# An adaLN decode block: attention in units of two kv heads, with fewer and larger loads

## The chip, the core and the metric

The kernel runs on one core of one Trainium2 chip. The core has a matrix engine (TensorE, PE in the profile, its weight loads PEld), a vector engine (VectorE, DVE), a scalar engine (ScalarE, ACT), a general engine (GpSimd, POOL) and a queue engine (SyncE, SP) that issues most transfers. Sixteen DMA engines move data between the main memory and the on-chip memory SBUF, which has 128 partitions. Matrix products land in a second memory, PSUM, and are read from there by DVE and ACT. Each engine runs its own instructions in the order in which they stand, and waits on semaphores for the others. The metric is the device time of one execution in microseconds (us), less is better.

## What is computed

Two tokens (B = 2, one position each) pass through an attention block and a feed-forward block. Both are modulated by a condition `c`. All numbers are float32.

```
mod = (silu(c) @ w_mod) -> sa, ca, ga, sb, cb, gb          # w_mod 512 x 3072
h = layernorm(x) * (1 + ca) + sa
q = h @ wq                                                 # 512 x 4096: 32 heads of 128
k, v = the last 4096 of 32768 cache rows, 8 kv heads       # 4 query heads share a kv head
o = softmax(q k^T / sqrt(128)) v ;  x = x + ga * (o @ wo)  # wo 4096 x 512
h = layernorm(x) * (1 + cb) + sb
x = x + gb * (silu(h @ w1) @ w2)                           # w1 512 x 1792, w2 1792 x 512
```

Nearly all bytes are read once: 16 pairs of batch and kv head, each with 2 MB of keys and 2 MB of values (67.1 MB), and 30.4 MB of weights, 97.5 MB in all.

## The kernel before

The kernel is written with a tile layer that makes the semaphores. Most instructions may be moved by its scheduler; those wrapped in `inorder(...)` keep the order in which they are written, on each engine.

**Loads.** All large loads go through SP's queue, in order. Their targets are tiles of a ring of eight (`RING = 8`, `stream()`), each 128 partitions by 16 KB, 2 MB. `load_rows` brings `w_mod` in four pieces and `wq` in four. `load_k` and `load_v` bring one head's keys or values of one batch: partition p holds 32 consecutive cache rows, 16 KB in one run. `load_runs` brings `wo`, `w1` and `w2`; the end of `w2` is cut into eight small pieces. A load may start when the ring's tile is free, that is, when the last reader of what lay there is done.

**Head.** `m_ch` and `m_sp` are products of `silu(c)` with `w_mod`, four of each per piece, as each piece lands. The queries (`q`, line 271) are 32 products of 512 columns, eight for each of the four pieces of `wq`. They are turned by DVE (`qT`, line 280), spread out (`qg`), repeated by a product (`qr`, line 288) and copied into `qbd` (line 294), the weights of the score products.

**Attention.** `seq` has 16 units t, one kv head of one batch each. For a unit:

- `keys` (line 352): DVE turns the keys in 32 x 32 blocks, four instructions of 128 x 1024, into `kT`.
- `scores` (line 368): 16 products of 256 columns into `s`. They stand in four groups of 32 output rows; products for different groups run side by side in the array.
- `maxima` (line 378): DVE takes each row's maximum `mx`; a product with the identity turns it into a row `mT` (line 460); `maxrow` reduces it (`mg`, line 384) and spreads it (`mrow`, line 390); a product (`bp`, line 398) makes a column of it, ACT copies it to `bias` (line 400).
- `exponentials` (line 402): ACT computes `pr = exp(scale * s + bias)` and its row sums.
- `turn` (lines 414, 416): DVE turns `pr` into `xp` and spreads it with a mask into `zp`.
- `permute` (lines 426, 433): four products gather it into `pT`, ACT copies that to `ptb`.
- `weighted` (lines 313, 322): eight products of 512 columns of values into `o`, in two parts of four; ACT copies `o` to `ob`.
- `collect` (line 328): four products of 128 columns, one for each group of output rows, add the unit's result to `o_all`.

The loop over t works on two units at a time: it turns the keys and makes the scores of unit t between the softmax and the weighting of unit t - 1. `kT` has two buffers (`ktp`, bufs=2), each of a whole unit.

**End.** The row sums give `lp` and `rl`; `on` and `oTn` are the scaled and turned result. `acc_o` (line 545, 24 products of 512 columns) and `ao` (line 554, 32 of 128) are the product with `wo`, joined by `gather` (line 532). Then follow the second layer norm in a transposed form (`aoT`, `x1T`, `mean`, `dT`, `hT`), the product with `w1` (`hid`, line 586), the activation (`hidT`, `z`, `sgh`, `uT`), the product with `w2` (`acc_yw`, line 619, and `acc_y`, line 629), two instructions for `yo`, and the store.

Of the kernel before, what the change touches and what calls it, by code (L numbers as in the profile page):

```python
# [16 lines left out]
G = HQ // HKV  # L17
F = 1792
EPS = 1e-5
RING = 8  # L20
# [3 lines left out]
def adaln_block(  # L24
# [19 lines left out]


# [4 lines left out]
    assert W == 4096  # L50


    head = ctx.enter_context(tc.tile_pool(name="head", bufs=1))
    id4 = head.tile([P, 32], F32, name="id4")
    ring = ctx.enter_context(tc.tile_pool(name="ring", bufs=RING))
# [5 lines left out]
    psum1 = ctx.enter_context(tc.tile_pool(name="psum1", bufs=1, space=bass.MemoryType.PSUM))  # L61

# [6 lines left out]
    def stream(name):  # L69
        return ring.tile([P, 4096], F32, tag="st", name=name)  # L70

    def load_rows(name, w, k, width):
        t = stream(f"{name}{k}")[:, :width]
        nc.sync.dma_start(t, w[k * P : (k + 1) * P, :])  # L74
        return t

    def load_k(b, h):
        t = stream(f"k{h}_{b}")
        nc.sync.dma_start(
            t, k_cache[b, h, SK - W :, :].rearrange("(p n) d -> p (n d)", p=P)  # L80
        )
        return t

    def load_v(b, h):
        t = stream(f"v{h}_{b}")
        nc.sync.dma_start(
            t, v_cache[b, h, SK - W :, :].rearrange("(p n) d -> p (n d)", p=P)
        )
        return t

    def load_runs(name, w, per, lo, hi):

        e = w.shape[1]
        t = stream(f"{name}{lo}")[:, : (hi - lo) * e].rearrange("p (q e) -> p q e", e=e)
        nc.sync.dma_start(t, w.rearrange("(p q) e -> p q e", q=per)[:, lo:hi, :])
        return t


    x2 = x.rearrange("b s d -> (b s) d")
    x_sp, x_ch, c_ch = const([P, P], "x_sp"), const([P, P], "x_ch"), const([P, P], "c_ch")  # L100
    for t in (c_ch, x_ch, x_sp):
        nc.vector.memset(t, 0.0)
    wm = [load_rows("wm", w_mod, 0, 6 * D)]
    rows8 = lambda t: t.rearrange("(ab r) m -> ab r m", r=16)[:, 0, :]
    for t, src in ((c_ch, c), (x_ch, x2)):
        for b in range(B):
            nc.sync.dma_start(
                rows8(t)[b : 2 * 4 : 2, :].rearrange("a (k c) -> a k c", k=4),
                src[b, :].rearrange("(k a c) -> a k c", k=4, a=4),
            )  # L110
# [61 lines left out]
    for t in ptb:  # L172
        nc.gpsimd.memset(t[:, P:], 0.0)
# [132 lines left out]
    def weighted(t, vt, part):  # L306


        if part == 0:
            o_ps[t] = bank("D", f"o{t}")  # L310
# [359 lines left out]
```

## Time and profile before

| quantity | value |
|---|---|
| median of 3 runs | 240.01 us (239.88 to 241.7) |
| span of the profiled execution, first to last instruction | 238.5 us |
| mean granted TensorE clock in it | 0.843 of full speed |
| records of PE | 1476, two for each of 738 float32 products |
| DVE, busy | 118.4 us, 212 instructions |
| ACT, busy | 35.2 us, 96 instructions |

The profile gives no time for the profiled execution other than its span; the median of the runs is 1.5 us above it, which stands for what lies around the span.

How to read what the prediction quotes: a page has the busy time of each engine, the span in 40 slices of 6 us (a digit is the busy share in tenths, PEclk the granted clock in tenths), the DMA queues, the chain of work that ended last, and the costliest groups of instructions. A row of a group reads: line, engine, operation, output <- input, shapes and count, then the busy time of the group in us and the mean of one in ns, then the idle time before them and what ended it. In rows of the timeline and of the chain the first number is the start in us from the span's start and the second the duration. "128\*32" is a product that takes 128 rows and 32 columns of the array.

### The profile page before, as it was taken

How to read it: one execution, taken by the hardware profiler on the slowest of the kernel's cores; microseconds unless marked ns; L12 is line 12 of the kernel's file. 1: busy time of each engine (PE TensorE's matmuls, PEld its weight loads, DVE VectorE, ACT ScalarE, POOL GpSimd, SP SyncE). 2: the span in 40 equal slices, each digit the busy share in tenths (PEclk: the TensorE clock that was granted, in tenths of full speed). 3: DMA queues.
4: the chain of work that ended last, by engine and by line, in shares of the span. 5: the costliest groups of instructions: out<-in, count | busy, mean ns of one | idle time of the engine just before them, and what ended most of it. 6: DMA issues, size and time to landing. Idle time of an engine off the chain costs nothing.

```text
span 238.5 us, 3514 instructions
## 1 busy us (share of the span) xinstructions
PE 163.8 (69%) x1476; PEld 64.3 (27%) x1476; DVE 118.4 (50%) x212; ACT 35.2 (15%) x96; POOL 9.3 (4%) x30
## 2 busy tenths in 40 slices
PE   0194656386987696787585967869759687776854
PEld 0131101122333132342231322414323131315212
DVE  0604001759687847649477485584864912101130
ACT  2300000103112202202112021120211211020200
POOL 8400000100000000000000000000000000000000
PEclk9999577766799977979979779797997897797779
DMA  6999999999999999999999999999999999999970
GB/s 243 428 429 431 431 429 440 426 427 431 426 434 431 423 434 426 434 429 434 426 429 434 430 426 431 431 429 430 426 431 430 429 437 426 420 430 425 419 247 20
DMA packets 7783, 97.75 MB, mean 410 GB/s; under 512 B 968, under 2 KB 984, under 8 KB 1752
## 3 DMA queue, kind: packets, MB, share of 16 engines
q1 hardware_dynamic: 7768, 97.54, 96.6%
q8 instruction: 11, 0.18, 0.3%
q14 instruction: 4, 0.03, 0.0%
HBM read 97.53 MB, written 0.00 MB: 409 GB/s over the span
## 4 chain that ended last, share of the span: by engine, by line
DMA 71%; DVE 17%; PE 8%; ACT 1%; issue 1%; SPq 1%; POOL 0%; POOLq 0%
DMA k<-in_A_k_cache_dram 42%; DVE kT L352 14%; DMA w<-in_B_w_dram 13%; DMA wq<-in_A_wq_dram 13%; PE s L368 4%; DMA wm<-in_w_mod_dram 3%; PE o L313 2%; DVE qT L280 1%; DVE mx L378 1%; SPq L74 1%; PE q L271 0%; DVE mrow L390 0%; DVE qbd L294 0%; PE pT L426 0%; DVE zp L416 0%
## 5 line engine op out<-in xcount | busy, mean ns | idle before, releaser
L352 DVE STREAM_TRANSPOSE kT<-k 128x1024 f32<-128x1024 f32 x64 | 75.5, 1215 | 16.0 <-DMA k<-in_A_k_cache_dram 16.0
L368 PE MATMUL s<-kT,qbd 128*32 128x256 f32 x512 | 69.7, 518 | 10.0 <-DVE kT L352 9.5
L313 PE MATMUL o<-v,ptb 128*32 128x512 f32 x256 | 35.2, 627 | 5.7 <-ACT ptb L433 5.7
L368 PEld LDWEIGHTS s<-kT,qbd 128*32 128x32 f32 x512 | 23.8, 140 | 46.5 <-DVE kT L352 29.9
L378 DVE TENSOR_REDUCE mx<-s 128x1 f32<-128x256 f32 x16 | 6.8, 425 | 30.0 <-PE s L368 30.0
L398 PE MATMUL bp<-negscale,mrow 1*128 1x1 f32 x32 | 6.5, 268 | 21.6 <-DVE mrow L390 21.6
L271 PE MATMUL q<-wq,hq_T 128*32 128x512 f32 x64 | 11.4, 847 | 9.7 <-DMA wq<-in_A_wq_dram 9.7
L322 ACT COPY ob<-o 128x512 f32<-128x512 f32 x16 | 9.4, 585 | 37.5 <-PE o L313 37.5
L398 PEld LDWEIGHTS bp<-negscale,mrow 1*128 1x128 f32 x32 | 5.1, 198 | 35.5 <-DVE mrow L390 35.5
L433 ACT COPY ptb<-pT 128x128 f32<-128x128 f32 x16 | 4.2, 265 | 66.1 <-PE pT L426 66.1
L328 PE MATMUL o_all<-ob,selh 128*32 128x128 f32 x128 | 13.2, 308 | 1.1 <-ACT ob L322 0.7
L426 PE MATMUL pT<-zp,id 128*32 128x128 f32 x128 | 13.5, 304 | 0.2 <-DVE zp L416 0.2
L416 DVE TENSOR_TENSOR zp<-xp,group 128x512 f32<-128x512 f32 x16 | 11.1, 693 | 0.5
L313 PEld LDWEIGHTS o<-v,ptb 128*32 128x32 f32 x256 | 7.8, 111 | 11.6 <-ACT ptb L433 10.3
L280 DVE STREAM_TRANSPOSE qT<-q 128x512 f32<-128x512 f32 x2 | 1.4, 717 | 18.8 <-PE q L271 18.5
L328 PEld LDWEIGHTS o_all<-ob,selh 128*32 128x32 f32 x128 | 8.0, 130 | 4.3 <-ACT ob L322 2.1
L426 PEld LDWEIGHTS pT<-zp,id 128*32 128x32 f32 x128 | 7.9, 127 | 1.0 <-issue 0.5
L402 ACT ACTIVATE pr<-s,bias 128x256 f32<-128x256 f32 x16 | 7.6, 474 | 0.7 <-ACT bias L400 0.2
L414 DVE STREAM_TRANSPOSE xp<-pr 128x256 f32<-128x256 f32 x16 | 6.4, 397 | 2.2 <-ACT pr L402 2.2
L271 PEld LDWEIGHTS q<-wq,hq_T 128*32 128x32 f32 x64 | 2.1, 130 | 19.0 <-DMA wq<-in_A_wq_dram 11.4
L545 PE MATMUL acc_o<-wo,oTn 128*32 128x512 f32 x48 | 6.9, 729 | 0.4 <-DVE oTn L523 0.4
L203 PE MATMUL mean_a<-mv_a,avg 128*128 128x1 f32 x2 | 0.6, 361 | 9.4 <-DVE mv_a L200 9.4
(126 smaller groups left out, 100.6 us busy)
## 6 DMA issues: line engine op xcount, KB each, us to landing
k<-in_A_k_cache_dram SPq DMA_DIRECT2D x16, 2048.0 KB
v<-in_A_v_cache_dram SPq DMA_DIRECT2D x16, 2048.0 KB
wq<-in_A_wq_dram SPq DMA_DIRECT2D x4, 2048.0 KB
wo<-in_A_wo_dram SPq DMA_DIRECT2D x4, 2048.0 KB
wm<-in_w_mod_dram SPq DMA_DIRECT2D x4, 1536.0 KB
w<-in_B_w_dram SPq DMA_DIRECT2D x2, 1024.0 KB
w<-in_B_w_dram SPq DMA_DIRECT2D x1, 1792.0 KB
w<-in_B_w_dram SPq DMA_DIRECT2D x2, 896.0 KB
```

What stands on the lines that cost most here:

```text
L271: nc.tensor.matmul(q_ps[n][32 * g : 32 * g + 32, :], hq_T[:, k, :], wv[:, n, g], start=(k == 0), stop=(k == 3),)
L313: inorder(nc.tensor.matmul(o_ps[t][32 * c : 32 * c + 32, :], ptb[t % 2][:, 16 * n : 16 * n + 32], vt[:, 512 * n : 512 * n + 512], start=(p ...
L322: inorder(nc.scalar.copy(sb_, o_ps[t]))
L328: inorder(nc.tensor.matmul(o_all[32 * m : 32 * m + 32, b, :], selh[:, m, HQ - G - G * h : 2 * HQ - G - G * h], o_sb[:, m * DH : (m + 1) * DH],
L352: inorder(nc.vector.transpose(kT[t][:, :, 8 * n4 : 8 * n4 + 8, :].rearrange("p j n k -> p n j k"), kt[t][:, n4 * 1024 : (n4 + 1) * 1024].r ...
L368: inorder(nc.tensor.matmul(s_ps[t][32 * cc : 32 * cc + 32, :], qbd[h // 4][:, h % 4, b, j, :], kT[t][:, j, 8 * cc : 8 * cc + 8, :], start= ...
L378: inorder(nc.vector.tensor_reduce(mx[t], s_ps[t], axis=AX.X, op=ALU.max))
L398: inorder(nc.tensor.matmul(bp[:, 0:1], mrow[t % 2], negscale, start=True, stop=True))
L402: inorder(nc.scalar.activation(pr[t].rearrange("p s k -> p (s k)"), s_ps[t], AF.Exp, bias=bias, scale=SCALE, accum_out=rowsum[:, h, b : b ...
L416: inorder(nc.vector.tensor_mul(zp, xp[:, None, :, 0:16].to_broadcast([P, 4, 8, 16]), group[:, :, None, None].to_broadcast([P, 4, 8, 16]),))
L426: inorder(nc.tensor.matmul(tp[32 * i : 32 * i + 32, :], id4, zp.rearrange("p c s x -> p (c s) x")[:, :, 4 * i : 4 * i + 4], start=True, st ...
L545: nc.tensor.matmul(acc[32 * g : 32 * g + 32, :], oTn[:, q, :], wot[q // 8][:, q % 8, :], start=(q < 4), stop=(q >= 20),)
```

## The change

The attention, its buffers and all large loads are written anew.

- **Buffers.** One tile `store` of 128 partitions by 144 KB replaces the ring. It holds four slots of 32 KB a partition (4 MB each) and a spare part for small tiles. At first `wq` lies in slots 0 and 1, and `w_mod` in slot 3 and the spare part.
- **Loads.** `w_mod` (6.3 MB) and `wq` (8.4 MB) are one load each. A unit is a batch and two kv heads, so there are 8 units; `load_cache` brings both heads' 4 MB at once: partition p holds 64 consecutive cache rows (one run of 32 KB) of head p mod 2. Keys of units 0, 2, 4, 6 go to slot 2 and values to slot 3; those of units 1, 3, 5, 7 to slots 0 and 1. `wo` is three loads, `w1` three, `w2` four of 128 partitions each. `x` and `c` come through ACT's queue, once each.
- **Head.** The products with `w_mod` and `wq` begin when the whole matrix has landed. The layer norm works on the same layout for both blocks, which saves a few small DVE instructions.
- **Attention.** `attend(t)` holds a whole unit, and the loop calls it for one unit after another; the part of unit t no longer stands between parts of unit t - 1. DVE turns the keys in four instructions of 128 x 2048. After each, four score products of 512 columns follow. They read `kT[:, 32f:32f+32, u:32:2]`, every second element, to pick head u. `kT` is now a quarter of a unit and has two buffers, so the third of the four instructions waits for the scores of the first. `mx`, `pr`, `xp` and the two `zp` work on 512 columns; `pT` has four products of 256 columns; `ptb` is made by two ACT instructions with a mask `par`; `o` has 16 products. After every second unit `o_all` gets four products of 256 columns that all write the same 32 output rows.
- **End.** `on` and `oTn` are made by DVE alone (`rq`, `on`, a reduction), without the four `oq` products. The rest is as before.

Of two engines it is shown how their order changes. First PE at the middle of the attention. Before, `s_415` are the scores of one unit, and `pT_375`, `o_381` belong to the unit ahead of the one whose scores are `s_355`:

```order
L398 MATMUL bp_343<-negscale,mrow_145 128x1
L368 MATMUL s_355<-kT_337,qbd_153 32x256 x16
L426 MATMUL pT_375<-zp_353,id_58 32x128 x4
L313 MATMUL o_381<-v_0_305,ptb_147 32x512 x4
L460 MATMUL mT_374<-ident,mx_372 1x128
L313 MATMUL o_381<-v_0_305,ptb_147 32x512 x4
L398 MATMUL bp_403<-negscale,mrow_146 128x1
L368 MATMUL s_415<-kT_397,qbd_153 32x256 x16
```

The same place on PE now, from the second unit (`s_341`) to the start of the third (`s_413`):

```order
L292 MATMUL s_341<-kT_342,qbd_124 32x512 x4
L292 MATMUL s_341<-kT_348,qbd_124 32x512 x4
L292 MATMUL s_341<-kT_354,qbd_124 32x512 x4
L292 MATMUL s_341<-kT_360,qbd_124 32x512 x4
L302 MATMUL mT_368<-ident,mx_366 1x128
L319 MATMUL bp_374<-negscale,mrow_121 128x1
L334 MATMUL pT_382<-store,sel 32x256 x4
L350 MATMUL o_389<-store 32x512 x16
L360 MATMUL o_all<-store,pick 32x256 x4
L292 MATMUL s_413<-kT_414,qbd_124 32x512 x4
```

Before, a unit's scores stand ahead of the weighting `o` of the unit before it; now all 16 products of `o`, and in every second unit the four of `o_all`, stand ahead of the next unit's first scores.

DVE before, where `mx_436` belongs to the unit with the keys `k_0_333` and everything with `xp` and `zp` to the unit ahead of it:

```order
L352 STREAM_TRANSPOSE kT_397<-k_0_333 128x8x4x32 x2
L414 STREAM_TRANSPOSE xp_411<-pr_407 128x256
L416 TENSOR_TENSOR zp_413<-xp_411,group 128x512
L378 TENSOR_REDUCE mx_436<-s_415 128x1
L352 STREAM_TRANSPOSE kT_461<-k_1_393 128x8x4x32 x2
L384 TENSOR_REDUCE mg_464<-mT_438 1x4
L390 COPY mrow_145<-mg_464 1x4x16
L352 STREAM_TRANSPOSE kT_461<-k_1_393 128x8x4x32 x2
```

DVE now, from the last turn of one unit's keys (`kT_292`) through that unit's softmax to the third turn of the next (`kT_354`); the tiles in `store` are `xp` and `zp`:

```order
L287 STREAM_TRANSPOSE kT_292<-store 128x2048
L300 TENSOR_REDUCE mx_298<-s_273 128x1
L304 TENSOR_REDUCE mg_302<-mT_300 1x8
L314 COPY mrow_120<-mg_302 1x2x16 x2
L325 STREAM_TRANSPOSE store<-store 128x512
L327 TENSOR_TENSOR store<-store,half 128x512 x2
L287 STREAM_TRANSPOSE kT_342<-store 128x2048
L287 STREAM_TRANSPOSE kT_348<-store 128x2048
L287 STREAM_TRANSPOSE kT_354<-store 128x2048
```

Before, DVE turns keys of the next unit while PE and ACT work on the maximum and the exponentials; now it goes through a unit's whole softmax, from `mx` to the second `zp`, before it turns any key of the next.

The diff, cut to the loads, the attention and the head's queries:

```diff
-RING = 8
+SLOT = 8192
...
+    store = big.tile([P, 36864], F32, name="store")
+    slot = [store[:, i * SLOT : (i + 1) * SLOT] for i in range(4)]
...
-    wm = [load_rows("wm", w_mod, 0, 6 * D)]
+    wm = store[:, 24576:36864].rearrange("p (k e) -> p k e", k=4)
+    nc.sync.dma_start(
+        wm.rearrange("p k e -> p (k e)"), w_mod.rearrange("(p k) e -> p (k e)", k=4)
+    )
...
-    wqt = [load_rows("wq", wq, k, HQ * DH) for k in range(4)]
+    wqt = store[:, :16384].rearrange("p (k e) -> p k e", k=4)
+    nc.sync.dma_start(
+        wqt.rearrange("p k e -> p (k e)"), wq.rearrange("(p k) e -> p (k e)", k=4)
+    )
...
+    def load_cache(cache, t, where):
+        hp, b = seq[t]
         nc.sync.dma_start(
+            where,
+            cache[b, 2 * hp : 2 * hp + 2, SK - W :, :].rearrange(
+                "u (i n) d -> i u (n d)", n=NK
+            ),
+        )
+        return where
...
+    def attend(t):
+        hp, b = seq[t]
+        s_ps = bank("A", f"s{t}")
+        kv = kt[t].rearrange("p (n j r) -> p n j r", n=NK, j=4)
         for j in range(4):
+            kT = ktp.tile([P, NK, 32], F32, tag="kT", name=f"kT{t}")
+            inorder(nc.vector.transpose(kT, kv[:, :, j, :]))
+            for u in range(2):
+                h = 2 * hp + u
+                for f in range(2):
+                    r = 32 * (2 * u + f)
+                    inorder(nc.tensor.matmul(
+                        s_ps[r : r + 32, :],
+                        qbd[h // 4][:, h % 4, b, j, :],
+                        kT[:, 32 * f : 32 * f + 32, u:32:2],
+                        start=(j == 0),
+                        stop=(j == 3),
+                    ))
...
         inorder(nc.scalar.activation(
+            pr, s_ps, AF.Exp, bias=bias, scale=SCALE, accum_out=rowsum[:, t : t + 1]
         ))
+        inorder(nc.vector.transpose(xp, pr))
+        for f in range(2):
+            inorder(nc.vector.tensor_mul(
...
+        for u in range(2):
+            inorder(nc.scalar.activation(
+                pt[:, :, u, :], tp.rearrange("p (n g) -> p n g", g=G), AF.Copy,
+                scale=par[:, u : u + 1],
+            ))
+        o_ps = bank("D", f"o{t}")
+        for i in range(16):
+            c_ = i % 4
+            inorder(nc.tensor.matmul(
+                o_ps[32 * c_ : 32 * c_ + 32, :],
+                ptb[t % 2][:, 32 * i : 32 * i + 32],
+                vt[t][:, 512 * i : 512 * i + 512],
+                start=(i < 4),
+                stop=(i >= 12),
+            ))
+        inorder(nc.scalar.copy(ob[:, b].rearrange("p n d -> p (n d)"), o_ps))
+        if b == B - 1:
+            for n in range(4):
+                inorder(nc.tensor.matmul(
+                    o_all[32 * hp : 32 * hp + 32, :, :],
+                    pick[:, n].rearrange("p w i -> p (w i)"),
+                    ob[:, :, n, :],
+                    start=(n == 0),
+                    stop=(n == 3),
+                    skip_group_check=True,
+                ))
...
+    where = [slot[i] for i in (2, 3, 0, 1)]
+    for t in range(2):
+        kt[t] = load_cache(k_cache, t, where[2 * t])
+        vt[t] = load_cache(v_cache, t, where[2 * t + 1])
+    for t in range(NP):
+        attend(t)
+        if t + 2 < NP:
+            kt[t + 2] = load_cache(k_cache, t + 2, where[2 * (t % 2)])
+            vt[t + 2] = load_cache(v_cache, t + 2, where[2 * (t % 2) + 1])
...
+    for lo, hi, s, at in ((0, 16, 2, 0), (16, 24, 3, 0), (24, 32, 3, 4096)):
+        wot |= load_rows(wo, 32, lo, hi, slot[s], at)
+    for lo, hi in ((0, 2), (2, 3), (3, 4)):
+        w1t |= load_rows(w1, 4, lo, hi, slot[0], lo * F)
+    WIDE = 8
+    for lo, hi in ((0, WIDE), (WIDE, 12), (12, 13), (13, 14)):
+        w2t |= load_rows(w2, T2, lo, hi, slot[1], lo * D)
```

429 lines of the change are left out of this document (141 added, 288 removed).

## Prediction

> **What bounds the kernel now.** I read the page from the top, then the chain of waits in order of time, then the groups, and last the timeline at the head and the tail. The page first: TensorE clock, DMA share and rate in 40 slices of 6 us, the queue of the large loads, and the chain by engine.
>
> ```profile
> span 238.5 us, 3514 instructions
> PEclk9999577766799977979979779797997897797779
> DMA  6999999999999999999999999999999999999970
> GB/s 243 428 429 431 431 429 440 426 427 431 426 434 431 423 434 426 434 429 434 426 429 434 430 426 431 431 429 430 426 431 430 429 437 426 420 430 425 419 247 20
> ...
> q1 hardware_dynamic: 7768, 97.54, 96.6%
> ...
> DMA 71%; DVE 17%; PE 8%; ACT 1%; issue 1%; SPq 1%; POOL 0%; POOLq 0%
> ```
>
> The loads bound the kernel: DMA is at its full share in every slice but the first and the last two, the rate is flat near 430 GB/s, and 71% of the chain is DMA. The span is 238.5 us; the median of the runs is 1.5 above it, which I add at the end. The next fence has, in the stretch of the attention, the busy time of PE, PEld, DVE, ACT and POOL with their counts, then the clock, the DMA share and the rate; behind it pieces of the chain (start, duration).
>
> ```profile
> 60.00:180.00 120.00, 90.68 (x864) 38.19 (x856) 81.21 (x115) 20.31 (x65) 0.00 (x0) 0.87 1.01 430
> 45.40 4.63 DVE kT L352 x4
> 148.89 2.28 DVE kT L352 x2
> 151.19 33.89 DMA k<-in_A_k_cache_dram
> 198.36 0.47 PE pT L426 x8
> 199.17 3.38 PE o L313 x16
> ```
>
> PE is busy for 90.7 of 120 us and DVE for 81.2. Neither is full, but they fit beside the loads only since work of two units overlaps. PE's clock is 0.87 even so. The keys of the last unit land at 185.08. Up to there `w_mod` (6.3 MB), `wq` (8.4), 16 loads of keys and 14 of values (2.1 each) have landed, 77.6 MB; at 430 GB/s that is 180.4 us, so a load lands 4.7 us behind its bytes divided by the rate. One unit of the changed kernel loads 8.39 MB: 19.5 us. The question is whether its chain of work can keep to 19.5.
>
> **The durations.** The groups of the attention (line, engine, operation, shapes, count, then the busy time in us and the mean in ns), and rows of the timeline that show the two speeds of PE:
>
> ```profile
> L378 DVE TENSOR_REDUCE mx<-s 128x1 f32<-128x256 f32 x16 | 6.8, 425 | 30.0 <-PE s L368 30.0
> L402 ACT ACTIVATE pr<-s,bias 128x256 f32<-128x256 f32 x16 | 7.6, 474 | 0.7 <-ACT bias L400 0.2
> L414 DVE STREAM_TRANSPOSE xp<-pr 128x256 f32<-128x256 f32 x16 | 6.4, 397 | 2.2 <-ACT pr L402 2.2
> L416 DVE TENSOR_TENSOR zp<-xp,group 128x512 f32<-128x512 f32 x16 | 11.1, 693 | 0.5
> L433 ACT COPY ptb<-pT 128x128 f32<-128x128 f32 x16 | 4.2, 265 | 66.1 <-PE pT L426 66.1
> L322 ACT COPY ob<-o 128x512 f32<-128x512 f32 x16 | 9.4, 585 | 37.5 <-PE o L313 37.5
> L460 PE MATMUL mT<-ident,mx 128*1 128x128 f32 x32 | 6.1, 272 | 0.5 <-DVE mx L378 0.5
> L398 PE MATMUL bp<-negscale,mrow 1*128 1x1 f32 x32 | 6.5, 268 | 21.6 <-DVE mrow L390 21.6
> L384 DVE TENSOR_REDUCE mg<-mT 1x4 f32<-1x64 f32 x16 | 2.8, 172 | 1.6 <-PE mT L460 1.6
> L390 DVE COPY mrow<-mg 1x64 f32<-1x64 f32 x16 | 2.9, 182 | 0.5
> L400 ACT COPY bias<-bp 128x1 f32<-128x1 f32 x16 | 2.6, 160 | 27.0 <-PE bp L398 27.0
> 28.12 3.52 PE L271 MATMUL q<-wq,hq_T 128*32 128x512 f32 x16 [2.23 <-DMA wq<-in_A_wq_dram]
> 39.38 1.92 PE L271 MATMUL q<-wq,hq_T 128*32 128x512 f32 x16 [1.41 <-DMA wq<-in_A_wq_dram]
> 41.92 0.72 DVE qT L280
> 193.65 1.07 PE o L313 x8
> 203.21 0.43 PE L328 MATMUL o_all<-ob,selh 128*32 128x128 f32 x8 [0.71 <-ACT ob L322]
> ```
>
> Sixteen records of 512 columns (eight products) took 3.52 us at 28.12, behind idle time, and 1.92 at 39.38. `o` shows the same: eight records in 1.07 at 193.65, sixteen in 3.38 at 199.17, where nothing was left to overlap. So a piece of PE work that follows a pause runs at about half speed, as the 5 in PEclk says.
>
> **The change, head.** `wq` lands as before (39.4: the same bytes ahead of it), but all 64 records of `q` now follow it, where 16 did. That is 7.7 us at the fast row, 14.1 at the slow one; I take 9.5, slow at first and fast then. The second `qT` then starts at 48.9, and from `qT` to the first turn of keys it is 3.5 as now (41.92 to 45.40): 52.4, which is 7 us later than today. Unit 0 has four turns of 2.25 each (a pair of today's takes 2.28), 9.0, then its softmax, 6.7 (below): 68.1. The keys of unit 1 land at the same time (27.3 MB / 430 GB/s + 4.7 = 68.1). I take 68.5 as the start of unit 1.
>
> **The change, one unit's cycle.** DVE goes in order. After the last `zp` of unit t it turns two quarters of the next keys, then must wait, since `kT` has two buffers: the third turn needs the scores of the first to be done, and on PE these stand behind `pT`, all of `o`, and in odd units `o_all`. From the last `zp`:
>
> - `pT`, four products of 256 columns; today 128 columns took 0.47 at the slow clock, so 0.5 fast to 0.9 slow: 0.7. `ptb`, two instructions for one of 0.265, each with twice the columns: 0.8.
> - `o`, 32 records: 4.3 at 1.07 for eight, 6.8 at 3.38 for sixteen. Ahead of it PE waits for the whole softmax, as it does ahead of the row at 199.17, so I take 6.0, near the slow end.
> - scores of the first quarter, eight records: 1.07 to 1.7, taken as 1.1; hops 0.15. Sum 8.75. The two free turns (4.5) are hidden under it.
> - Third and fourth turn: 4.5.
> - Softmax: last scores 1.3; `mx` of 512 columns 0.7 (under twice 0.425); `mT` 0.4 and `bp` 0.4 (two overlapping records of 0.27 each); `mg` and two `mrow` 0.5; `bias` 0.2; `pr` of 512 columns with its sum 0.8 (`ob`, as wide, has 0.585); `xp` 0.7 (as `qT`); two `zp` 1.4; hops 0.3. Sum 6.7. All of it is in a row now; before, turns of keys lay between its steps.
>
> An even unit's cycle is 8.75 + 4.5 + 6.7 = 19.95. After an odd one `ob` (0.6) and `o_all` come in between. Four products of 256 columns write the same 32 rows, which no row of this trace shows: if they run side by side as now, twice 0.43 = 0.9; if one after another, eight records of half the columns of the `q` rows, where four side by side took 0.48 or 0.88: 1.9 fast, 3.5 slow. I take 1.9, since PE comes warm from `o`; odd cycle 22.45. The mean is 21.2, over the 19.5 of the loads. The bound moves from DMA to this chain through DVE, PE and ACT.
>
> The Trainium skill, TensorEngine Tiling (Array Packing), section Key Properties, says that different tiles of the array work in parallel. By it the four products on one tile's columns lose this, which is the serial case; the parallel one would make the forecast 3 us less.
>
> Starts of DVE's turns: unit 1 at 68.5, then 88.45, 110.9, 130.85, 153.3, 173.25, unit 7 at 195.7. Its keys land at 185.1 (the same 77.6 MB ahead), so it runs 10.6 behind the loads. Its last `zp` is at 215.65; `pT`, `ptb`, `o`, `ob`, `o_all` and hops, 10.15, end at 225.8 (today 203.6).
>
> **The change, tail.** Rows of the timeline, each with its start, which give the steps by their differences:
>
> ```profile
> 203.71 0.61 DVE L517 TENSOR_SCALAR on<-o_all,rl 128x128 f32<-128x128 f32 x2 [5.32 <-PE o_all L328]
> 205.90 6.94 PE L545 MATMUL acc_o<-wo,oTn 128*32 128x512 f32 x48 [0.36 <-DVE oTn L523]
> 215.77 1.93 PE L554 MATMUL ao<-wo,oTn 128*32 128x128 f32 x32 [2.92 <-DMA wo<-in_A_wo_dram]
> 219.63 0.32 DVE L564 STREAM_TRANSPOSE aoT<-ao 128x128 f32<-128x128 f32 x1 [5.13 <-PE ao L554]
> 221.62 2.38 PE L586 MATMUL hid<-w,hT_b 128*32 128x448 f32 x16 [0.46 <-DVE hT_b L577]
> 226.96 0.65 DVE L603 STREAM_TRANSPOSE hidT<-hid 128x448 f32<-128x448 f32 x1 [1.94 <-PE hid L586]
> 229.43 3.56 PE L619 MATMUL acc_yw<-w,uT 128*32 128x512 f32 x16 [2.55 <-DVE uT L615]
> 235.24 0.29 DVE L639 TENSOR_TENSOR yo<-acc_y,mod_sp 128x128 f32<-128x128 f32 x1 [5.92 <-PE acc_y L629]
> ```
>
> `on` and the reduction that replaces `oq` cost 1.0 (0.61, and 0.43 as `mx`); `acc_o` 6.94; `ao` with gather 3.86 (to 219.63); the norm 1.99; `hid` 5.34; the activation 2.47; `acc_yw` 3.56; `acc_y` 2.25; `yo` and store 3.26: 30.7. In `hid` and `acc_y` short waits for loads are left in. End 225.8 + 30.7 = 256.5, with 1.5 **258**. `w2`'s slot is free when the last `o` is done, about 222; its 3.7 MB take 8.5 and the 4.7, landing at 236, and are wanted at 247: hidden. `wo` and `w1` are there long before.
>
> **Costed at nothing.** Fewer transfers and runs of 32 KB: today's rate is flat with 96.6% of the queue's share, so at most some 2 us of DMA time are to be had, and DMA no longer ends last. With four slots, the values of unit t + 2 can start only when `o` of unit t is done, 28 after that unit's start (a cycle and 7.5 for `pT`, `ptb`, `o`); the keys of unit t + 3 come behind them and land at 28 + 19.5 + 4.7 = 52, wanted at 3 x 21.2 = 63.6: hidden by 11. If the cycle were shorter than 19.5, this cover and that of the fewer transfers would go, and the loads would end last as today. The products with `w_mod`, the saved small DVE instructions and the move of `x` and `c` to ACT's queue lie under the load of `wq`.
>
> The Trainium skill, DMA: Bandwidth & Descriptors, section Latency and other measured facts, puts a fixed cost of about 2 us on a transfer: 34 fewer would be 68 us if they stood in a row. The flat GB/s line shows no gaps between them, so the trace does not bear this out here.
>
> **The rivals.**
>
> 1. *PE stays at its fast clock, and the loads still end last.* Then `o` is 4.3 and `o_all` 0.9, the cycles 18.25 and 19.75, 19.0 in the mean, and unit 7 starts when its keys land, 185.1; 18.25 + 7.45 + 30.7 behind that is 241.5, with 1.5 243. With a fast tail too (`acc_o` 5.8 at 1.92 for sixteen, `hid` 3.5, `acc_yw` 1.9) it is 238, and if unit 7 doesn't wait for `o` ahead of it, 235.5. No slower than now. For it: 0.87 now. Against: PE would be busy for some 13 of 21 us with a pause of 6.7 for the softmax, and the row at 199.17 shows `o` behind such a pause. It decides below a cycle of 19.5. Chance 0.12.
> 2. *Reading every second element halves the score products.* Then each quarter's scores take 1.2 more, of which the first and the last lie in the cycle: 2.4 for each of 7 cycles, 17 in all: 275. All operands of products before are read in runs of four elements or more, so no row speaks. Chance 0.10.
> 3. *The two heads of a load, 16 MB apart for neighbouring partitions, halve its rate.* All loads here run at 430 whether 12 or 16 KB lie together, and none has such a step. At half rate 67.1 MB take 156 us more, and the loads end last: 395. Chance 0.03. The Trainium skill, DMA: Bandwidth & Descriptors, section Latency and other measured facts, reports half the rate where partitions lie 4 or 8 MB apart in memory; there all 128 stepped so, here two do, and no run here shows it yet.
> 4. *The forecast*, 248 to 268, chance 0.75: its low end has `o` and `o_all` near the fast rows, its high end `o` 6.8, `o_all` 3.5 and `q` 14.1.
>
> **The numbers.** 258 us, range 247 to 272: the forecast's own spread and a part of the second rival; rivals 1 and 3 and the upper part of 2 are left out. About 1% is what can be told from no change. Faster 0.04 (rival 1 with a fast tail and no wait for `o`), within 1% 0.06 (most of the rest of it), slower 0.90 (forecast 0.75, rival 2 0.10, rival 3 0.03, and 0.02 of rival 1, at 243).
>
> **What would show it.** DVE's idle time ahead of the turns would be ended by PE's scores, no longer by `k` loads, and the chain would be mostly DVE and PE. The starts of the first turns would be 52 and then about 21 us apart, alternating by 2.5. `o` would take near 6, `o_all` near 1.9, first-quarter scores about 1.1 (2.2 or more for rival 2). DMA would show gaps in the second half and 430 GB/s where it runs (rival 3: 215). The time from the last `o_all` to the end would be 31. I am wrong if turns still wait for loads, or if units are 19.5 apart or less: then the cycle is shorter than I think, and first of all `o` is faster.

## The result, and the profile after

| kernel | median of 4 runs, us | lowest to highest | ratio to before, 95% interval |
|---|---|---|---|
| before | 240.5 | 239.88 to 241.7 | |
| changed | 256.81 | 255.9 to 257.02 | 1.066 (1.062 to 1.070) |

The changed kernel is 6.6% slower; forecast was 258 in a range of 247 to 272. Some executions ran in a slower state with a lower clock; the times and ratios here leave them out (two of four runs of c1_warm and one of twelve of e1_kt4_2mb, below). Its span is 254.8 us, 2.0 below the median. First the page: clock, DMA share and rate in 40 slices (now of 6.4 us), the queue of the loads, the chain by engine.

```profile
span 254.8 us, 2424 instructions
PEclk9999956967577569657756965875696587579999
DMA  7999899999999999999999999899999989979100
GB/s 270 472 412 494 381 432 419 417 442 442 427 421 432 437 432 422 437 437 430 417 442 432 435 412 448 314 406 422 399 422 412 413 332 424 418 263 401 68 0 3
...
q1 hardware_dynamic: 4044, 97.52, 90.3%
...
PE 46%; DVE 20%; DMA 14%; issue 11%; ACT 7%; SPq 0%; DVEq 0%; ACTq 0%
```

And for the stretch from 60 to 180 us the busy time of PE, PEld, DVE, ACT and POOL, then the clock, the DMA share and the rate:

```profile
60.00:180.00 120.00, 70.84 (x424) 17.30 (x420) 67.45 (x64) 14.87 (x36) 0.00 (x0) 0.68 0.99 425
```

DMA has fallen from 71% of the chain to 14%, and PE, DVE and ACT hold 73%. The loads still run at some 420 to 440 GB/s in most slices, but from the 26th slice on some have 314, 332 and 263: the loads pause there. PE is busy for 70.8 of 120 us (before 90.7) at a clock of 0.68 (before 0.87). So less work per microsecond, at a lower clock: an engine that waits. The groups say for whom (busy time, mean in ns, idle time ahead and what ended it; the first row is that of the kernel before, the others are of the changed one):

```profile
L352 DVE STREAM_TRANSPOSE kT<-k 128x1024 f32<-128x1024 f32 x64 | 75.5, 1215 | 16.0 <-DMA k<-in_A_k_cache_dram 16.0
L287 DVE STREAM_TRANSPOSE kT<-store 128x2048 f32<-128x2048 f32 x32 | 71.9, 2288 | 38.0 <-PE s L292 36.7 <-DMA store<-in_A_k_cache_dram 1.3
L292 PE MATMUL s<-kT,qbd 128*32 128x512 f32 x256 | 43.7, 748 | 22.3 <-DVE kT L287 22.3
L350 PE MATMUL o<-store 128*32 128x512 f32 x256 | 44.5, 860 | 7.6 <-ACT store L343 7.6
L334 PE MATMUL pT<-store,sel 128*32 128x256 f32 x64 | 8.7, 632 | 25.7 <-DVE store L327 25.7
```

Before, DVE's turns of keys idled 16.0 us, all for loads. Now they idle 38.0, of which 36.7 end with `s` on PE, the scores of the first quarter; only the first wait of the second unit, 1.3, is for a load. The chain in order of time shows a unit from `pT` on (start, duration, what):

```profile
111.14 1.12 PE pT L334 x8
112.28 0.85 ACT store L343 x2
113.17 5.66 PE o L350 x32
118.83 0.97 PE s L292 x7
119.86 2.20 issue
122.06 2.28 DVE kT L287
124.39 1.98 PE s L292 x8
...
127.14 0.60 PE mT L302 x2
...
130.68 1.31 DVE store L327 x2
...
139.64 0.59 ACT store L357
140.28 1.27 PE o_all L360 x5
```

Everything is in one row. The third turn (shown as "issue" at 119.86, the fourth as `kT` at 122.06) begins when the first quarter's scores end at 119.80, and these follow `o`. DVE's first two turns began at 110.91 and were done at 115.4: 4.4 us of idle time. The units' first turns start at 50.6, 68.5, 87.8, 110.9, 131.9, 155.0, 176.1 and 199.2, which is 19.3, 23.1, 21.0, 23.1, 21.1 and 23.1 us apart from the second on (the first of these began 1.3 late, behind its load), 21.8 in the mean. The longer ones have `ob` and `o_all` in them. The loads' pace is 19.5.

The end, in rows of the timeline:

```profile
228.92 1.91 PE L360 MATMUL o_all<-store,pick 128*32 128x256 f32 x8 [0.77 <-ACT store L357]
230.87 0.42 DVE L415 TENSOR_TENSOR on<-o_all,rq 128x256 f32<-128x256 f32 x1 [10.31 <-PE o_all L360]
231.97 5.36 PE L440 MATMUL acc_o<-store,oTn 128*32 128x512 f32 x48 [1.14 <-DVE oTn L420]
...
247.66 1.92 PE L511 MATMUL acc_yw<-store,uT 128*32 128x512 f32 x16 [2.54 <-issue]
...
251.48 0.29 DVE L531 TENSOR_TENSOR yo<-acc_y,mod_sp 128x128 f32<-128x128 f32 x1 [3.92 <-PE acc_y L521]
```

From the end of `o_all` at 230.8 it takes 24.0 us, where before it was 34.9 with waits for loads. The clock in this stretch is 0.98, before it was 0.80.

### The profile page after: what moved, and what is told of

The parts are those of the page before. It is cut to its first block, busy times and chain, and to the rows that moved or that the text cites. A ratio compares the mean times of both kernels' runs of the same rounds, so it can differ in the third digit from the quotient of the medians.

```text
span 254.8 us, 2424 instructions
## 1 busy us (share of the span) xinstructions
PE 144.2 (57%) x1012; PEld 40.5 (16%) x1012; DVE 113.6 (45%) x155; ACT 29.1 (11%) x64; POOL 7.1 (3%) x27
## 4 chain that ended last, share of the span: by engine, by line
PE 46%; DVE 20%; DMA 14%; issue 11%; ACT 7%; SPq 0%; DVEq 0%; ACTq 0%
PE o L350 18%; DMA store<-in_A_wq_dram 14%; PE s L292 9%; DVE kT L287 8%; DVE store L327 4%; PE q L242 4%; PE pT L334 4%; ACT store L343 3%; PE o_all L360 3%; ACT store L322 2%; DVE store L325 2%; DVE mx L300 2%; PE acc_o L440 2%; PE mT L302 2%; PE bp L319 2%
## 5 line engine op out<-in xcount | busy, mean ns | idle before, releaser
L287 DVE STREAM_TRANSPOSE kT<-store 128x2048 f32<-128x2048 f32 x32 | 71.9, 2288 | 38.0 <-PE s L292 36.7
L292 PE MATMUL s<-kT,qbd 128*32 128x512 f32 x256 | 43.7, 748 | 22.3 <-DVE kT L287 22.3
L350 PE MATMUL o<-store 128*32 128x512 f32 x256 | 44.5, 860 | 7.6 <-ACT store L343 7.6
L334 PE MATMUL pT<-store,sel 128*32 128x256 f32 x64 | 8.7, 632 | 25.7 <-DVE store L327 25.7
L350 PEld LDWEIGHTS o<-store 128*32 128x32 f32 x256 | 9.9, 153 | 42.0 <-issue 27.3
L292 PEld LDWEIGHTS s<-kT,qbd 128*32 128x32 f32 x256 | 7.6, 115 | 48.4 <-DVE kT L287 41.1
L242 PE MATMUL q<-store,hq_T 128*32 128x512 f32 x64 | 9.3, 745 | 9.1 <-DMA store<-in_A_wq_dram 9.1
L327 DVE TENSOR_TENSOR store<-store,half 128x512 f32<-128x512 f32 x16 | 10.4, 688 | 0.2
L343 ACT ACTIVATE store<-pT,par 128x256 f32<-128x256 f32 x16 | 6.7, 470 | 26.8 <-PE pT L334 26.8
L360 PE MATMUL o_all<-store,pick 128*32 128x256 f32 x32 | 7.7, 382 | 2.9 <-ACT store L357 2.9
```

The costliest lines, as they stand in the source:

```text
L242: nc.tensor.matmul(q_ps[n][32 * g : 32 * g + 32, :], hq_T[:, k, :], wv[:, n, g], start=(k == 0), stop=(k == 3),)
L287: inorder(nc.vector.transpose(kT, kv[:, :, j, :]))
L292: inorder(nc.tensor.matmul(s_ps[r : r + 32, :], qbd[h // 4][:, h % 4, b, j, :], kT[:, 32 * f : 32 * f + 32, u:32:2], start=(j == 0), stop= ...
L327: inorder(nc.vector.tensor_mul(zp[:, 32 * f : 32 * f + 32, :].rearrange("p (s y) w -> p s y w", y=2), xp[:, :, None, 0:16].to_broadcast([P ...
L334: inorder(nc.tensor.matmul(tp[32 * a : 32 * a + 32, :], sel, zp[:, :, 4 * a : 4 * a + 4], start=True, stop=True,))
L343: inorder(nc.scalar.activation(pt[:, :, u, :], tp.rearrange("p (n g) -> p n g", g=G), AF.Copy, scale=par[:, u : u + 1],))
```

## The experiments

Eleven kernels were run. Each was timed beside the kernel before on the same chip; the last column is the ratio to it with its 95% interval.

| kernel | edit | us | ratio to before |
|---|---|---|---|
| a1_kt3 | changed, three buffers for `kT` | 236.91 | 0.988 (0.983 to 0.993) |
| a1_kt4 | changed, four buffers for `kT` | 236.56 | 0.985 (0.981 to 0.988) |
| b1_before_serial | before, one unit after another | 285.62 | 1.189 (1.184 to 1.193) |
| c1_warm | changed, idle products in PE's pauses | 275.69 | 1.147 (1.142 to 1.153) |
| c2_warm | the same, eleven of the products moved behind the exponentials | 240.31 | 1.002 (0.999 to 1.005) |
| d1_after_pipe | changed, order of before | 251.40 | 1.043 (1.039 to 1.048) |
| e1_kt4_2mb | a1_kt4, loads of 2 MB at most | 240.70 | 0.999 (0.997 to 1.002) |
| e2_kt4_cut | a1_kt4, `w2` in ten pieces | 238.70 | 0.993 (0.991 to 0.995) |
| g1_contig | changed, no step in the score operand | 254.83 | 1.062 (1.059 to 1.065) |
| j1_pause | changed, a pause ahead of the end | 268.10 | 1.115 (1.110 to 1.120) |
| h1_kt4_w2two | a1_kt4, `w2` in two loads | 238.08 | 0.992 (0.990 to 0.994) |

**The wait of the third turn.** One word of the changed kernel is edited:

```diff
-    ktp = ctx.enter_context(tc.tile_pool(name="ktp", bufs=2))
+    ktp = ctx.enter_context(tc.tile_pool(name="ktp", bufs=3))
```

> One more buffer for kT (three). Theory, the wait of the third turn for scores that stand behind o: now only the fourth turn waits, the cycle of a unit (21.0 after even units and 23.1 after odd ones in the changed kernel) is 2.3 shorter, 19.8 in the mean, seven cycles 16 us less: 240 to 243, with the loads nearly the bound again. Rival, the 4 MB loads into four slots can't come faster: 255 to 258. Rival, the slow PE clock sets the cycle wherever the turns stand: 250 or more.

With four, room is made elsewhere (the diff without the small tiles):

```diff
-    ktp = ctx.enter_context(tc.tile_pool(name="ktp", bufs=2))
+    ktp = ctx.enter_context(tc.tile_pool(name="ktp", bufs=4))
...
-    ptb = [spare[:, 1024 + 512 * i : 1536 + 512 * i] for i in range(2)]
+    ptb = [spare[:, 1024:1536]] * 2
```

> Four buffers for kT; to make room, ptb has one buffer and three small tiles of the head and the end share its second place. Theory of the wait: no turn waits for PE, the cycle is about 17.3 (19.7 after odd units), under the 19.5 of the loads, which end last again: the last unit starts when its keys land, at 185, its o_all ends at 211, and the end waits for w2: 236 to 240. Rival, the loads in 4 MB pieces are the bound: 255 to 258. Three buffers and four apart by over 4 us would say that the loads are not the bound at three.

236.91 and 236.56 us: the whole loss is gone, 20 us (19 by the ratios) for a buffer of 8 KB a partition, and both kernels are a little faster than the one before, by 1.2 and 1.5%. With three buffers the time is even 3 below what was expected. I had counted seven cycles, but the wait goes in the last unit too: from its first turn to the end of `o_all` that unit takes 26.8 us, in the changed kernel 31.6. The group of the turns with three buffers:

```profile
L287 DVE STREAM_TRANSPOSE kT<-store 128x2048 f32<-128x2048 f32 x32 | 71.7, 2287 | 24.6 <-DMA store<-in_A_k_cache_dram 19.2 <-PE s L292 5.4
```

Turns in its timeline, with what ended the idle time ahead of them:

```profile
125.97 6.70 DVE L287 STREAM_TRANSPOSE kT<-store 128x2048 f32<-128x2048 f32 x3 [3.58 <-DMA store<-in_A_k_cache_dram]
133.66 2.31 DVE L287 STREAM_TRANSPOSE kT<-store 128x2048 f32<-128x2048 f32 x1 [0.98 <-PE s L292]
145.41 8.89 DVE L287 STREAM_TRANSPOSE kT<-store 128x2048 f32<-128x2048 f32 x4 [3.04 <-DMA store<-in_A_k_cache_dram]
```

And with four buffers, from the second unit to the last:

```profile
67.88 8.89 DVE L286 STREAM_TRANSPOSE kT<-store 128x2048 f32<-128x2048 f32 x4 [1.18 <-DMA store<-in_A_k_cache_dram]
87.23 8.89 DVE L286 STREAM_TRANSPOSE kT<-store 128x2048 f32<-128x2048 f32 x4 [4.06 <-DMA store<-in_A_k_cache_dram]
...
184.38 8.89 DVE L286 STREAM_TRANSPOSE kT<-store 128x2048 f32<-128x2048 f32 x4 [3.23 <-DMA store<-in_A_k_cache_dram]
```

With three, DVE waits 19.2 of 24.6 us for loads of keys and the fourth turn waits a little for `s`. With four, all four turns of a unit are one piece of 8.89 us, each begun by a load, 19.4 us apart: the pace of the loads, which I had at 19.5. The two kernels are 0.35 us apart, so with three the loads are the bound already. The rival that 4 MB loads can't come faster falls, and so does the one that the slow clock sets the cycle wherever the turns stand.

**The order alone.** The kernel before, with its loads, its ring and its two whole-unit buffers for `kT`, goes through one unit after another:

```diff
-    for t in range(NP + 1):
-        u, last, now = t - 1, t > 0, t < NP
...
+    for t in range(NP):
+        fetch(t + 1)
+        for n4 in range(4):
+            keys(t, n4)
+        scores(t)
+        maxima(t)
...
+        zp = turn(t)
+        permute(t, zp)
+        weighted(t, vt[t], 0)
+        o_sb[t] = weighted(t, vt[t], 1)
+        collect(t, seq[t][1], seq[t][0], o_sb[t])
```

> The kernel before, its loads and buffers as they are, with one unit after another: turns, scores, softmax, o, o_all of unit t, then unit t + 1. Theory, the order makes the loss: a cycle is 4.6 for the turns, 2.5 for the scores, 3.7 for the softmax, 10.8 against 9.75 of the loads, so sixteen units end some 16 us later, part of which the shorter end gives back: 244 to 252. Rival, the order costs nothing beside loads of 2 MB and the loss of the changed kernel comes from its large loads and slots: 239 to 242.

285.62 us, 45 more than before: the sign was right and the size far too small. A unit takes 10.9 to 13.6 us, 12.7 in the mean of thirteen, not 10.8. I had let the turns of the next unit (4.6) stand for the time between two softmaxes, but it is PE that fills it. In the timeline of this kernel:

```profile
108.39 4.62 DVE L352 STREAM_TRANSPOSE kT<-k 128x1024 f32<-128x1024 f32 x4
...
109.66 3.64 PE L313 MATMUL o<-v,ptb 128*32 128x512 f32 x16 [0.38 <-ACT ptb L433]
113.36 0.59 ACT L322 COPY ob<-o 128x512 f32<-128x512 f32 x1 [3.76 <-PE o L313]
114.00 0.66 PE L328 MATMUL o_all<-ob,selh 128*32 128x128 f32 x8 [0.70 <-ACT ob L322]
114.43 3.64 PE L368 MATMUL s<-kT,qbd 128*32 128x256 f32 x32
```

The turns are done at 113.0, yet the scores start at 114.43 behind `o`, `ob` and `o_all`, and both `o` and `s` take 3.64 at a slow clock (eight of these sixteen records of `o` took 1.07 before). The cycle is the whole row from `pT` to `zp`, and with small units it is paid sixteen times: the order alone can cost more than the changed kernel lost. With units twice as large it is paid eight times, and a1_kt4, in the same order, shows that it then fits under the loads once no turn waits for PE.

**The clock.** Products of 128 columns, which nobody reads, are put into PE's pauses:

```diff
+        def warm(t_, n):
+            for _ in range(n):
+                inorder(nc.tensor.matmul(
+                    t_[:, 256:384], ident, mean512, start=True, stop=True, skip_group_check=True
+                ))
...
+        warm(mT, 3)
...
+        warm(bp, 2)
...
+        warm(bp, 12)
         bias = work.tile([P, 1], F32, tag="bias", name=f"bias{t}")
...
+        warm(bp, 3)
         o_ps = bank("D", f"o{t}")
```

> The changed kernel with 20 products of 128 columns in each unit that nobody reads, in the pauses of PE during the softmax. Theory of the wait with the clock as its second part: PE stays at the fast clock, o takes 4.3 for 5.5, pT 0.6 for 1.1, the last scores 1.0 for 1.9, mT and bp 0.4 for 0.6, so the cycle is 3 us shorter, 19.0 in the mean: 240 to 245. If busy products don't raise the clock, or the clock isn't what makes them slow: 256 to 260, with the dummy products only in the way.

275.69: slower by 19, since `bias` read the tile that the twelve products had just written and so waited for all of them (2.9 us in each unit). The try tells nothing about the sum, but in its fastest unit `o` took 3.92 (5.53 in the slowest) and the last scores 1.10. The second try puts the eleven of that pause behind the exponentials, and two for three ahead of `o`:

```diff
-        warm(bp, 12)
         bias = work.tile([P, 1], F32, tag="bias", name=f"bias{t}")
...
+        warm(mT, 11)
         inorder(nc.vector.transpose(xp, pr))
...
-        warm(bp, 3)
+        warm(mT, 2)
         o_ps = bank("D", f"o{t}")
```

> As the kernel with products that nobody reads, but with the eleven that fill the pause of the exponentials issued behind the exponentials (before, the bias waited for them, 2.9 us in each unit). Theory, the clock is the second part of the loss: the fast durations that the first try showed, o 3.9 for 5.5, last scores 1.1 for 1.9, mT and bp 0.38 for 0.6, come with nothing in the way: the cycle is 18.5 to 19.5 in the mean, 237 to 244. If it stays over 250, the time that the clock gives is lost to waits that I have not seen.

The stretch from 60 to 180 us, columns as above, and a unit in the timeline:

```profile
60.00:180.00 120.00, 96.20 (x735) 46.58 (x728) 74.85 (x72) 16.41 (x40) 0.00 (x0) 0.97 1.00 430
```

```profile
116.62 1.10 PE L292 MATMUL s<-kT,qbd 128*32 128x512 f32 x8 [1.09 <-DVE kT L287]
...
123.03 0.64 PE L343 MATMUL pT<-store,sel 128*32 128x256 f32 x8 [0.48 <-DVE store L336]
...
124.63 3.64 PE L360 MATMUL o<-store 128*32 128x512 f32 x32 [0.32 <-ACT store L352]
126.07 4.50 DVE L287 STREAM_TRANSPOSE kT<-store 128x2048 f32<-128x2048 f32 x2 [3.10 <-DMA store<-in_A_k_cache_dram]
...
131.86 4.50 DVE L287 STREAM_TRANSPOSE kT<-store 128x2048 f32<-128x2048 f32 x2 [1.28 <-PE s L292]
```

240.31. The clock is 0.97 for 0.68, `o` takes 3.64 for 5.66, `pT` 0.64 for 1.08, the last scores 1.10 for 1.94 (rows of the timeline of both), and the whole loss of 16 us is gone, with more work on PE. These three alone make 3.3 us in the unit shown. The third turn still waits for `s` (1.28 us ahead of 131.86), but the first one waits for the loads again (3.10 ahead of 126.07).

Does the wait of the third turn make the low clock? The stretch and two rows of a1_kt4, where no turn waits for PE:

```profile
60.00:180.00 120.00, 75.23 (x488) 20.53 (x484) 74.33 (x72) 16.42 (x40) 0.00 (x0) 0.76 1.00 432
...
102.68 1.08 PE L333 MATMUL pT<-store,sel 128*32 128x256 f32 x8 [3.22 <-DVE store L326]
104.71 6.20 PE L349 MATMUL o<-store 128*32 128x512 f32 x32 [0.95 <-ACT store L342]
```

For the most part it doesn't. The clock is 0.76, `o` takes 5.0 to 6.2 us over the units, and the pause ahead of `pT` is 3.2 us, as in the changed kernel (in c2_warm 0.48). So the softmax, which now stands in a row, still pauses PE, and the rows stay slow. The loss took both: a turn that waits behind `o`, and an `o` that is slow. Either cure is enough to bring the cycle down to the pace of the loads: one more buffer with a slow `o`, or a fast `o` with two buffers. The Trainium skill, TensorE: Matmul & The Clock Gate, section Part 1: The HAM clock gate, has it that the slow clock is what an idle array gets and that a few microseconds of steady work lift it; 0.68 and 0.97 for the same work without and with the idle products agree.

**The order of before in the changed kernel.** With two `kT` buffers, `attend` is split, and the loop runs as the old one did:

```diff
-    for t in range(NP):
-        attend(t)
+    for t in range(NP + 1):
+        u, last, now = t - 1, t > 0, t < NP
+        if now:
+            scores(t, (0, 1))
+        if last:
+            expo(u)
+        if now:
+            scores(t, (2, 3))
+        if last:
+            turn(u)
...
+        if last:
+            permute(u)
+            weighted(u, 0, 8)
+        if now:
+            maxt(t)
+        if last:
+            weighted(u, 8, 16)
+            collect(u)
```

> The changed kernel, two buffers for kT, its parts put in the order of the kernel before: turns and scores of unit t, with the softmax of unit t - 1 between them, then pT and o of unit t - 1 around the mT of unit t. If the order alone makes the loss: 236 to 241. Rival, the four slots of 4 MB: o of unit t is done some 18.7 us after the keys of unit t + 1 land, so the values of unit t + 2 start 4 us late in the stream, a unit takes about 21.5 us and the loads show gaps: 245 to 252.

251.40 in the median, 248.62 in the profiled run: the rival's time. The turns' group; then, in time, the end of `o`, the load of values that goes out right behind it with the next keys behind that, and turns of two units:

```profile
L290 DVE STREAM_TRANSPOSE kT<-store 128x2048 f32<-128x2048 f32 x32 | 71.8, 2282 | 58.7 <-DMA store<-in_A_k_cache_dram 58.7
```

```profile
102.34 1.88 PE L366 MATMUL o<-store 128*32 128x512 f32 x13
104.30 0.53 SPq L93 DMA_DIRECT2D store<-in_A_v_cache_dram  x1
104.93 0.56 SPq L93 DMA_DIRECT2D store<-in_A_k_cache_dram  x1
106.84 4.51 DVE L290 STREAM_TRANSPOSE kT<-store 128x2048 f32<-128x2048 f32 x2 [7.59 <-DMA store<-in_A_k_cache_dram]
...
127.97 4.50 DVE L290 STREAM_TRANSPOSE kT<-store 128x2048 f32<-128x2048 f32 x2 [9.09 <-DMA store<-in_A_k_cache_dram]
```

DVE's turns never wait for PE any more (58.7 us, all for `k`). But the values' slot is free only when `o` is done, and that now stands behind all scores of the next unit: the load of the fourth unit's values goes out at 104.30, which in the changed kernel it did at 95.39. The next keys go out behind it at 104.93, and the turn that waits for them starts at 127.97, 21.1 after the one at 106.84. Seven starts from 67.75 to 191.06 give 20.6 in the mean, against 21.5 expected. So the old order and the big slots don't go together: four slots hold two units, and a read that ends some 9 us later keeps the next load out. That smaller slots would cure it was not tried.

**The size of the loads**, which the forecast put at 2 us at most, off the path. a1_kt4 makes the loads the bound, and so lets it be priced:

```diff
-        nc.sync.dma_start(
-            where,
-            cache[b, 2 * hp : 2 * hp + 2, SK - W :, :].rearrange(
-                "u (i n) d -> i u (n d)", n=NK
-            ),
-        )
+        src = cache[b, 2 * hp : 2 * hp + 2, SK - W :, :].rearrange("u (i n) d -> i u (n d)", n=NK)
+        for r in (slice(0, 4096), slice(4096, 8192)):
+            nc.sync.dma_start(where[:, r], src[:, :, r])
```

and `w_mod`, `wq` and the first load of `wo` are cut alike.

> The kernel with four kT buffers (236.6), with all loads over 2 MB cut into pieces of 2 MB or 1.5 MB, runs of 16 or 12 KB as before the change. The four buffers let the loads end last, so this is what the size of the loads is worth: the last load landed at 229.6 with large ones and at 234.7 in the kernel before. If the size gave these 5 us: 240 to 242. If it gives nothing, as the prediction had it within 2 us: 236 to 238.

Ratio 0.999 for 0.985: the smaller loads cost 3.5 us (0.0147 of 240; 2.1 to 5.0 between the ends of the two intervals). Each partition's run of bytes in a load is shorter too, so the two are not told apart. Where in the span the time lies stays open. The other part is the last weight:

```diff
-    for lo, hi in ((0, WIDE), (WIDE, 12), (12, 13), (13, 14)):
-        w2t |= load_rows(w2, T2, lo, hi, slot[1], lo * D)
+    for lo, hi in ((0, 4), (4, WIDE)):
+        w2t |= load_rows(w2, T2, lo, hi, slot[1], lo * D)
...
+    for lo, hi, cuts in (
+        (WIDE, 11, (0, 128)),
+        (11, 12, (0, 104, 128)),
+        (12, 13, (0, 112, 126, 128)),
+        (13, 14, (0, 120, 128)),
+    ):
```

> The kernel with four kT buffers (236.6), with w2 cut as before the change, two pieces of 1 MB and eight small ones of some partitions each, for four. If these pieces are what let the last load land 5 us later before the change: 239 to 242. If they are harmless or help the end: 235 to 237.

238.70, 2.1 more (0.7 to 3.3 between the ends of the two intervals), which lies between the two expectations. In a1_kt4 the last wait for `w2` ends at 229.63, here at 232.12. And fewer:

```diff
-    for lo, hi in ((0, WIDE), (WIDE, 12), (12, 13), (13, 14)):
+    for lo, hi in ((0, WIDE), (WIDE, T2)):
```

> The kernel with four kT buffers (236.6), w2 in two loads, rows 0 to 8 and 8 to 14, for four. Ten pieces cost 2.1 us against four. If each further piece costs about 0.3: 236.0. If the products of the last rows now wait for one larger load: 236.5 to 237.5.

238.08, which is over both expectations. `acc_y` in a1_kt4 and in this kernel:

```profile
229.76 0.86 PE L520 MATMUL acc_y<-store,uT 128*32 128x128 f32 x24 [0.58 <-DMA store<-in_B_w_dram]
```

```profile
231.01 0.86 PE L520 MATMUL acc_y<-store,uT 128*32 128x128 f32 x24 [1.73 <-DMA store<-in_B_w_dram]
```

It starts 1.25 later: the products of row 8 now wait for the one load of rows 8 to 14. Four loads were the best of the three ways.

**The step of two in the score operand**, the prediction's second rival:

```diff
-                        kT[:, 32 * f : 32 * f + 32, u:32:2],
+                        kT[:, 32 * f : 32 * f + 32, 16 * u : 16 * u + 16],
```

> The changed kernel with score products that read 16 columns in a row of each block of kT, in place of every second of 32: the choice of the head by the step is left out, so the scores mix both heads. Rival of the prediction, a step of two halves the rate: the eight records of a quarter would take 0.5 for 1.0 to 1.1 and the time would fall by about 7 x 1.5, to 246. Theory, the step costs nothing: s records as before, 255 to 258.

254.83, just under the expected span of times; its interval (1.059 to 1.065) overlaps that of the changed kernel (1.062 to 1.070). Eight records at a fast clock take 1.06 us where they took 1.11 with the step. A step of two costs at most 5% of the scores, not half of their rate.

**The end.** Its rows in the kernel before added up to 30.7, and it took 24.0. Were they slow by the clock, or by waits for loads?

```diff
+    inorder(nc.vector.memset(idle[0], 0.0))
+    inorder(nc.vector.tensor_copy(
+        idle[0][:, : B * DH].rearrange("p (b d) -> p b d", b=B), o_all
+    ))
+    for i in range(3):
+        inorder(nc.vector.transpose(idle[(i + 1) % 2], idle[i % 2]))
```

> The changed kernel with a pause of 7.3 us ahead of the end: DVE copies o_all and turns a tile of zeros three times before it may make on, and nobody reads that. It asks why the end took 24 us and not the 31 taken from the rows of the kernel before. If those rows were long because PE came to them cold, PE is cold behind the pause and the end takes 1.5 to 6 more than the pause itself: 265.5 to 270. If they were long only by waits for loads, it costs the pause alone: 263.5 to 264.5.

```profile
239.05 0.39 DVE L422 TENSOR_TENSOR on<-o_all,rq 128x256 f32<-128x256 f32 x1
...
240.12 7.45 PE L447 MATMUL acc_o<-store,oTn 128*32 128x512 f32 x48 [8.49 <-DVE oTn L427]
...
258.10 3.56 PE L518 MATMUL acc_yw<-store,uT 128*32 128x512 f32 x16 [2.53 <-issue]
```

268.10: 11.3 more than the changed kernel, 3.9 more than the pause of 7.4 (`on` starts at 239.05, behind an `o_all` that ends at 231.63). The four runs lie between 265.24 and 268.72, which is 1.0 to 4.5 beside the pause. `acc_o` takes 7.45 for 5.36 and `acc_yw` 3.56 for 1.92, which is 3.7 of the 3.9. With all weights there, these are the durations of the kernel before and more (6.94 and 3.56): those two rows were slow by the clock. The pause right ahead of a row does not settle its speed alone: `acc_yw` stands behind 2.5 us of idle time in the kernel before, in the changed one and here, and takes 3.56, 1.92 and 3.56. `ao` and `hid` stay as short as in the changed kernel (1.05 for 1.06 a row of `ao`); what made them longer before, a wait for loads or the clock, the pause doesn't tell.

## Why the prediction was right

*The bound moves from the loads to the chain through DVE, PE and ACT.* Shown: DVE's waits for `s` (36.7 of 38.0 us), and a third buffer for `kT` that takes 20 us off, by the very wait that the prediction named. The loss also needs slow PE rows, as rival 1 had it: c2_warm takes it away and leaves `kT` its two buffers.

*The cycle of a unit.* Forecast 19.95 and 22.45, measured 21.0 and 23.1 (the first, 19.3). Its terms, from the rows of the chain above: `pT` 1.1 for 0.7, `ptb` 0.85 for 0.8, `o` 5.3 to 5.9 for 6.0, first scores 1.0 for 1.1, the two turns 4.5 as forecast, last scores 2.0 for 1.3, `mT` and `bp` 0.6 each for 0.4, the other steps within 0.1. So `o` was a little too long and all the short PE pieces too short. I had seen that PE behind a pause runs at half speed and used it in full for `o` alone. `pT`, the last scores, `mT` and `bp` stand behind pauses just as well.

*The head.* `q` took 9.3 for 9.5, the first turn started at 50.6 for 52.4, the second unit at 68.45 for 68.5, behind its keys. The first turn was early since `wq`, in one load, landed early: `q` starts at 37.71, where the forecast had 39.4 as in the kernel before. c2_warm and a1_kt4 have the second unit at 67.9, at or just behind its keys, so the later head cost little or nothing.

*The last `o_all`* ended at 230.8 for 225.8, five late by the cycles; `o_all` itself took 1.91 for 1.9, four products on one group of rows, one after another.

*The end.* 24.0 for 30.7. This is the term that was mis-sized most. Its rows come from a stretch at a clock of 0.80, with waits for weights; in the changed kernel 32 records of `o` and eight of `o_all` stand directly ahead, no load is awaited, and the clock is 0.98. `acc_o` with `ao` took 7.5 for 10.8, `hid` 3.7 for 5.3, `acc_yw` with `acc_y` 3.8 for 5.8. In the sum `acc_o` and `acc_yw` together are too long by 3.2, and j1_pause shows that a pause alone makes these two as long; for the rest, clock and waits for loads are not told apart. That an error of +5 and one of -6.7 nearly cancelled is luck; either alone would still have been inside the range.

*Costed at nothing.* In the changed kernel no turn behind the second unit's first waits for a load, so the size of the loads is off the path in the attention, as forecast. But the flat rate had hidden what it is worth: where the loads are the bound it is 3.5, not 2 at most, and `w2` in four loads gives 2.1 more. The slots cost nothing, as forecast. Their spare time is needed, though: in d1_after_pipe, where the values go out some 9 us later, every unit from the second on waits 7 to 10 us for its keys.

*The rivals.* The fast clock that holds the pace of the loads (rival 1, 0.12) doesn't occur by itself: 0.68. Made by force in c2_warm it gives 240.3, within the 235.5 to 243 worked out for it. The step (rival 2) costs nothing to speak of. The two heads 16 MB apart (rival 3) run at some 430 GB/s in the first half of the attention. The Trainium skill, DMA: Bandwidth & Descriptors, section Latency and other measured facts, gives half the rate for a pitch of 4 or 8 MB between partitions; two streams 16 MB apart show none of it here (432 GB/s from 60 to 180 us in a1_kt4).

## What to carry to other kernels

When units get bigger, look for the buffer that held a whole unit and now holds a part: the engine that fills it waits for the reader, whose own queue decides for how long; here one more buffer was worth 20 us, and the gain of the larger loads showed only once it was there. Price each piece of PE work by the pauses around it where it will stand, not where its row stood, and where rows at both speeds exist, carry both through the sum. Before work is moved behind other work, count when each slot of the loads comes free.

## What had not been expected of the hardware

- With the loads as the bound, cutting loads of 4 to 8 MB into pieces of 1.5 to 2 MB cost 3.5 us of 240 (2.1 to 5.0), though the rate of the kernel before, with such pieces, looked flat at 430 GB/s.
- The granted clock follows PE's own pauses: 0.68 in the changed kernel, 0.76 with four `kT` buffers, 0.97 with idle products in the pauses (all from 60 to 180 us). A pause of 7.4 us ahead of the end made `acc_o` and `acc_yw` 3.7 us longer, and `acc_yw` starts more than 10 us behind that pause.
